# Fourier steps 48 to 127 as 64-row matmuls on both row halves, early maxima as head pairs among them

## The chip, the core and the metric

The program runs on one core of a Trainium2 chip. A core has TensorE (matmuls, with weight loads that run beside them; "PE" and "PEld" in the profile), VectorE (DVE), ScalarE (ACT), GpSimd (POOL) and SyncE (SP), which here only issues DMAs. TensorE writes to PSUM, eight banks of 128 x 512 floats; the other engines read PSUM (GpSimd does not here) and the on-chip memory. Each engine takes its instructions in the order of its own queue, and waits on semaphores for the others. The metric is the device time of one execution in microseconds, lower is better.

## What is computed

Two identical layers; each is a Fourier mixing block and then multi-query attention with 32 heads of 16 columns and one shared key and value head. S = 2048 rows, D = 512 columns.

```python
x = x + _A_ref(_layernorm(x), ...)      # a = x @ dft_hid_re.T ; b = x @ dft_hid_im.T
                                        # y = dft_seq_re @ a - dft_seq_im @ b
x = x + _B_ref(_layernorm(x), ...)      # q = x @ wq (32 heads) ; k = x @ wk ; v = x @ wv
                                        # softmax(q k^T / 4) v, then @ wo
```

The kernel does both blocks twice (two layers).

## The kernel before

**Precision.** A product of two float32 matrices is done in three matmuls on rounded parts: high x high, high x low, low x high (mm3, L86 to L89). Splitting a tile is a cast on ScalarE and a subtraction on VectorE or GpSimd (split_sb, split_ps, split_act, L70 to L84).

**The Fourier stage** (phase_a, L501) first multiplies along the sequence. There are four row blocks tb of 512 output rows, and for each block a cosine part (c = 0) and a sine part (c = 1) of 16 steps s: step n = 32 tb + 16 c + s multiplies the row tile s of the normalised input (xnh, xnl, kept for all 16 tiles) with a 128 x 512 tile of the cosine or sine matrix (ch, cl, loaded and split some steps ahead by c_load and c_split, four buffers each). The result has four 128-column parts d, each in a bank of its own (z, four banks from two pair() tiles); a step is four times mm3, twelve matmuls of 512 columns over all 128 rows. The last sixteen steps work on halves of 256 columns. After step 15 of a part the four z banks are split into zh and zl, and after both parts four y tiles of 128 rows (y_tile, L385: 24 matmuls into one y bank, then an add, a store and statistics on VectorE) finish the block.

**Preparing queries, keys and values.** While the next block's steps run, the twelve steps after a block's y tiles carry its preparation as tasks, one group behind each step (prep_tasks, L469): layer norm (alloc, ln_apply on GpSimd), four transposes (tr_tile, L246, into the single z-tagged bank, then split_act), keys and values (kv, L256), and four query projections (q_mm, L278), each with a weight split just ahead (wq_split) and six stores to DRAM (q_store). A query tile i (128 rows, 32 heads as 16 pairs) lies in DRAM as qd[i]: rows 0 to 63 belong to the even head of a pair and rows 64 to 127 to the odd one (48 rows used, 16 zero). qT_load brings it into one of the big buffers (slot) as o.qT[i].

**Maxima.** Softmax needs the row maximum of the scores of each head. For every query tile, pair, head g and key block kb of 512 keys this is one matmul (queries as weights, keys as the moving operand) into a y bank and one reduce_max on VectorE. There are three y banks (L65), shared with y_tile, kv, q_mm and the transposed maxima. Keys are kept twice: kz[0] has the keys on rows 0 to 63 and zeros below, kz[1] the other way round. In attention max_half (L344) uses the 64 rows of the head alone. In the Fourier stage max_one (L332) uses all 128 rows with the zero-padded kz[g], so that all matmuls there have one row mode. EARLY (L35) lists which (query tile, key block) is done in the Fourier stage: (i, kb, buffer, step of the load or None, begin, end). Begin and end are in units of which a block has 40: 32 steps, and 8 for its four y tiles (two per y tile, so a unit has four places both in steps and in y tiles). The 32 maxima of an entry are spread evenly over its units, put at quarters (after each d of a step, or after each three matmuls of a y tile; the dictionary inner).

**Attention** (phase_b, L833): per step four score matmuls of 64 rows (score, L681), their exponentials on ScalarE (L701), the product with the values (pv, L705) and on average three more maxima, taken from the list units, which leaves out what EARLY has done.

Of the kernel before, what the change touches and what calls it, by code (L numbers as in the profile page):

```python
# [17 lines left out]
P = 128  # L18
S = 2048
# [28 lines left out]
def fnet_mqa_kernel(ctx: ExitStack, tc: tile.TileContext, x_in, ct, dt_, wq, wkv, wo, out):  # L48
# [66 lines left out]
    def qd_zero(t):  # L115
        for g in range(2):
            nc.gpsimd.dma_start(qd[t, 64 * g + M0:64 * g + 64, :], f(kz[0][64:64 + 64 - M0, :]))
# [69 lines left out]
    def make_layer(L, src, mid, dst, last):  # L187
# [49 lines left out]
        def wq_split(g):  # L237
            st["wqh", g] = hl_tiles()
            split_sb(st["wq", g], *st["wqh", g], nc.gpsimd)
# [16 lines left out]
        def kv(t0, n, xth, xtl, vt=None):  # L256
            pk = bank("y")[:, :n * P]
            for k in range(NK):
                mm3(pk, wkvh[:, k, :], wkvl[:, k, :], xth[:, k, :n * P], xtl[:, k, :n * P], k == 0, k == NK - 1)
            cs = slice(t0 * P, (t0 + n) * P)  # L260
            if vt is None:
                vt = half(7)[:64, :n * P]
            nc.scalar.copy(vt[32:64], pk[32:64])
            for g in range(2):
                gs = slice(64 * g, 64 * g + 64)
                nc.scalar.activation(kz[g][gs, cs], pk[gs], AF.Identity, scale=kmask[gs], bias=kone[gs])
            for g in range(2):
                gs = slice(64 * g + 32, 64 * g + 48)
                nc.vector.tensor_sub(kz[g][gs, cs], pk[gs], f(kz[g][gs, cs]))
            return vt  # L270
# [61 lines left out]
        def max_one(i, pr, g, c0, n, to):  # L332
            pm = bank("y")[:, :n]
            nc.tensor.matmul(pm, o.qT[i][:, pr, :], kz[g][:, c0:c0 + n], start=True, stop=True)  # L334
            nc.vector.reduce_max(to, pm, axis=AX.X)  # L335

        def max_early(e, pr, g):
# [3 lines left out]
            to = st["mxe"][:, KEPT.index(EARLY[e]), pr, g:g + 1] if i else partial(0)[:, pr, g, kb:kb + 1]  # L341
            max_one(i, pr, g, kb * 512, 512, to)

        def max_half(i, pr, g, kb):  # L344
            pm = bank("y")
            gs = slice(64 * g, 64 * g + KR)
            nc.tensor.matmul(pm, o.qT[i][gs, pr, :], kz[g][gs, kb * 512:kb * 512 + 512], start=True, stop=True)  # L347
            nc.vector.reduce_max(partial(i)[:, pr, g, kb:kb + 1], pm, axis=AX.X)  # L348
# [120 lines left out]
        def prep_tasks(tb, x1):  # L469
# [20 lines left out]
            ts[5] = [do_kv]  # L490
            ts[6] = [lambda: wq_split(0), lambda: v_tr(4 * tb, 4, st["vt"])]
# [9 lines left out]
        def phase_a(extra):  # L501
# [8 lines left out]
            if L == 0:  # L510
                for n in range(NT):
                    add(n, lambda n=n: ln_step(n))
                add(20, load_wkv)
                for t in range(NT):
                    add(20 + 2 * t, lambda t=t: qd_zero(t))
# [5 lines left out]
            inner = {}  # L521
            for e, (i, kb, k, n0, n1, n2) in enumerate(EARLY):
                if n0 is not None:
                    add(n0, lambda i=i, k=k: qT_load(i, k))
                for u in range(2 * NPAIR):
                    at = divmod(int(4 * (n1 + u * (n2 - n1) / (2 * NPAIR))), 4)
                    b, n = divmod(at[0], 40)
                    at = (32 * b + n, at[1]) if n < 32 else ("y", b, 4 * (n - 32) + at[1])
                    inner.setdefault(at, []).append(lambda e=e, u=u: max_early(e, u // 2, u % 2))
            zh, zl, x1, vt = {}, {}, {}, {}  # L530
            z = None
# [15 lines left out]
            def maxes(c0, sl):  # L547
                for pr in range(HALF):
                    for g in range(2):
                        yield lambda pr=pr, g=g: max_one(0, pr, g, c0, 256, partial(0)[:, pr, g, sl:sl + 1])  # L550
# [33 lines left out]
            for n in range(125, 128):  # L584
                for d in range(NK):
                    inner[n, d] = [lambda: take(ma, 1)]
            add(124, lambda: wq_all(0))
            add(126, lambda: (wq_all(1), wq_split_pool(0), wq_split_pool(1)))
            add(127, lambda: (wq_split_pool(2), wq_split_pool(3)))
            for n in range(128):  # L590
# [3 lines left out]
                if s == 0:  # L594
                    za, zb = pair(), pair()
                    z = [za[:, 0, :], za[:, 1, :], zb[:, 0, :], zb[:, 1, :]]
                    if n == 112:
                        z = [z[d % 4][:, 256 * (d // 4):256 * (d // 4) + 256] for d in range(8)]
# [7 lines left out]
                ch, cl = hls.pop(n)  # L606
                for d in range(NK):
                    dsl = slice(d * P, (d + 1) * P)
                    if n < 112:
                        mm3(z[d], xnh[:, s, dsl], xnl[:, s, dsl], ch, cl, s == 0, s == NT - 1)  # L610
                        if s == 15 and d % 2:
                            for e in (d - 1, d):
                                raw = [half(6 + e % 2)] if c or e < d else []
                                (split_act if raw else split_ps)(z[e], zh[c][:, e, :], zl[c][:, e, :], *raw, neg=c == 1)
                    else:
                        h, sp = divmod(n - 112, 8)
                        zd = z[4 * h + d]
                        for j in range(2):
                            js = slice(256 * j, 256 * j + 256)
                            mm3(zd, xnh[:, 2 * sp + j, dsl], xnl[:, 2 * sp + j, dsl], ch[:, js], cl[:, js],  # L620
                                sp + j == 0, sp + j == 8)
                        if sp == 7 and d % 2:
                            hs = slice(256 * h, 256 * h + 256)
                            for e in (d - 1, d):
                                split_ps(z[4 * h + e], zh[c][:, e, hs], zl[c][:, e, hs], neg=c == 1)
                    for fn in inner.pop((n, d), ()):
                        fn()
# [24 lines left out]
            for g in range(4):  # L652
                q_half(14, g, *xt[1], lambda: take(mb, 2 if g else 0))
# [27 lines left out]
        def score(i, s_, j):  # L681
# [7 lines left out]
            if i == NT - 1 and jj == 1 and o.done == len(units):  # L689
                e = bank("y")  # L690
                nc.tensor.matmul(e, kz[g][64 * g:64 * g + KR, c * P:(c + 1) * P],
# [6 lines left out]
            nc.tensor.matmul(st["e"][:, g, :], kz[g][64 * g:64 * g + KR, c * P:(c + 1) * P],  # L698
# [248 lines left out]
```

## Time and profile before

| | us |
|---|---|
| median of three runs | 3772.63 (3770.57 to 3775.99) |
| the profiled execution, first to last instruction | 3768.5 |
| Fourier stage of layer 0, to step 44 / from step 45 | 190.76 / 513.94 |
| attention of layer 0 | 1185.90 |
| Fourier stage of layer 1, to step 44 / from step 45 | 177.50 / 509.90 |
| attention of layer 1 | 1190.50 |

One stretch of layer 0, the steps 76 to 95, with the busy time of each engine:

```profile
376.20:464.50 88.30, 86.51 (x370) 67.98 (x369) 81.36 (x133) 16.60 (x29) 28.65 (x23) 1.00 0.33 107
```

The row gives begin, end and length of the stretch, then for each engine in the order PE, PEld, DVE, ACT, POOL its busy us and number of instructions, then the clock that TensorE was granted (1.00 is full), the mean share of the DMA engines in use, and GB/s. In rows of the timeline the first two numbers are start and duration, then engine, source line, operation, out<-in, shape (rows * columns of the array for TensorE) and count; brackets hold the idle time of the engine before it and what ended it. A matmul's duration is longer than its slot, because matmuls are pipelined: the distance of starts is its cost.

### The profile page before, as it was taken

To read this page: it belongs to the slowest core of one execution; us is meant where nothing else is said; L and a number is where in the kernel's file an instruction comes from. 1 tells how busy PE (TensorE), PEld (TensorE's weight loads), DVE (VectorE), ACT (ScalarE), POOL (GpSimd) and SP (SyncE) were. 2 spreads that over 40 slices of the span, in tenths; PEclk is the share of its full clock that TensorE was granted. 3 is DMA by queue.
4 is the path that set the end of the run, shared out by engine and by line. 5 is a ranking of instruction groups with operands and counts; after the bars stand their busy time and mean duration, and the time that the engine had idled before them with its cause. 6 is when DMAs were issued, how large, how long until landed. Compare 5 with 4: busy or idle time off the path is not lost.

```text
span 3768.5 us, 56828 instructions
## 1 busy us (share of the span) xinstructions
PE 3662.8 (97%) x21826; PEld 1982.0 (53%) x21826; DVE 2804.0 (74%) x4743; ACT 2371.4 (63%) x2846; POOL 831.8 (22%) x1009
## 2 busy tenths in 40 slices
PE   8989999999999999999999999999999999999999
PEld 6777778633433333333377777785334333333433
DVE  5165978688888888888411769777888888888882
ACT  3212211588888888888933221216888888888888
POOL 5634342211111111111155343421000000000000
PEclk9999999999999999999999999999999999999999
DMA  5543332311111100110133342413111111001100
GB/s 181 122 136 103 99 97 88 98 34 37 42 35 33 50 21 21 33 49 21 41 129 103 112 126 76 123 60 99 33 49 32 35 35 44 24 21 49 33 23 25
DMA packets 204704, 242.51 MB, mean 64 GB/s; under 512 B 36880, under 2 KB 160784, under 8 KB 197264
## 3 DMA queue, kind: packets, MB, share of 16 engines
q1 hardware_dynamic: 199504, 222.08, 19.6%
q0 software_dynamic: 4864, 16.78, 1.6%
q8 instruction: 171, 2.80, 0.3%
q14 instruction: 101, 0.83, 0.1%
q10 hardware_dynamic: 64, 0.02, 0.0%
HBM read 174.58 MB, written 63.17 MB: 63 GB/s over the span
## 4 chain that ended last, share of the span: by engine, by line
PE 82%; DVE 4%; ACT 3%; issue 3%; POOL 2%; DMA 1%; SPq 0%; POOLq 0%; ACTq 0%; DVEq 0%
PE z L712 25%; PE x L698 18%; PE y L347 11%; PE y L334 6%; PE x L87 5%; PE x L89 5%; PE x L88 5%; PE y L87 3%; DVE mxp L348 3%; PE y L89 2%; PE y L88 2%; ACT slot L701 1%; POOL row L182 1%; POOL cl L79 1%; POOL slot L84 1%
## 5 line engine op out<-in xcount | busy, mean ns | idle before, releaser
L701 ACT ACTIVATE slot<-x 128x1024 f32<-128x1024 f32 x1990 | 1942.9, 1027 | 334.8 <-PE x L698 267.1
L348 DVE TENSOR_REDUCE mxp<-y 128x1 f32<-128x512 f32 x3040 | 1908.7, 684 | 280.6 <-PE y L347 228.4
L712 PE MATMUL z<-slot,v 128*32 128x512 f32 x8192 | 1096.2, 605 | 1.9 <-ACT row L715 1.9
L698 PE MATMUL x<-slot,kz 64*128 64x512 f32 x2956 | 900.4, 446 | 4.4 <-DMA slot<-mt 3.8
L698 PEld LDWEIGHTS x<-slot,kz 64*128 64x128 f32 x2956 | 375.1, 185 | 732.1 <-ACT slot L701 597.9
L347 PE MATMUL y<-kz,slot 64*128 64x512 f32 x2272 | 747.8, 436 | 4.7 <-ACT mt L378 0.7
L335 DVE TENSOR_REDUCE mxe<-y 128x1 f32<-128x512 f32 x832 | 525.2, 684 | 122.7 <-PE y L334 121.7
L87 PE MATMUL x<-ch,xnh 128*128 128x512 f32 (+1 forms) x1152 | 432.6, 376 | 12.9 <-ACT xnh L449 8.5
L89 PE MATMUL x<-ch,xnl 128*128 128x512 f32 (+1 forms) x1152 | 429.7, 373 | 1.2 <-POOL xnl L450 0.7
L88 PE MATMUL x<-cl,xnh 128*128 128x512 f32 (+1 forms) x1152 | 427.9, 371 | 0.4 <-POOL cl L79 0.4
L334 PE MATMUL y<-kz,slot 128*128 128x512 f32 (+1 forms) x1088 | 380.4, 399 | 43.6 <-DMA slot<-qd 15.3
L752 POOL TENSOR_TENSOR row<-row,row 128x256 f32<-128x256 f32 x63 | 46.2, 734 | 1679.6 <-DMA row<-rd 971.3
L347 PEld LDWEIGHTS y<-kz,slot 64*128 64x128 f32 x2272 | 359.3, 185 | 99.0 <-DVE mxp L348 29.6
L78 ACT CAST ch<-craw 128x512 fp32r<-128x512 f32 x256 | 156.4, 619 | 387.9 <-PE x L89 366.0
L79 POOL TENSOR_TENSOR cl<-craw,ch 128x512 fp32r<-128x512 f32 x236 | 307.8, 1310 | 361.4 <-ACT ch L78 295.4
L712 PEld LDWEIGHTS z<-slot,v 128*32 128x32 f32 x8192 | 163.5, 108 | 276.7 <-issue 248.6
L334 PEld LDWEIGHTS y<-kz,slot 128*128 128x128 f32 x1088 | 203.3, 190 | 106.6 <-DVE mxe L335 27.4
L87 PEld LDWEIGHTS x<-ch,xnh 128*128 128x128 f32 x1152 | 219.5, 191 | 52.9 <-ACT xnh L449 8.5
L88 PEld LDWEIGHTS x<-cl,xnh 128*128 128x128 f32 x1152 | 219.3, 190 | 43.5 <-POOL cl L79 0.7
L89 PEld LDWEIGHTS x<-ch,xnl 128*128 128x128 f32 x1152 | 218.7, 190 | 44.6 <-POOL xnl L450 4.5
L335 DVE TENSOR_REDUCE mxp<-y 128x1 f32<-128x512 f32 (+1 forms) x256 | 146.0, 619 | 126.5 <-PE y L334 125.8
L87 PE MATMUL y<-slot,slot 128*128 128x512 f32 x384 | 156.6, 408 | 8.9 <-DVE mxp L348 5.8
(144 smaller groups left out, 2837.3 us busy)
## 6 DMA issues: line engine op xcount, KB each, us to landing
craw<-ct_in SPq DMA_DIRECT2D x112, 512.0 KB
slot<-qd SPq DMA_DIRECT2D x44, 1024.0 KB
qd<-row SPq DMA_DIRECT2D x144, 128.0 KB
od<-row SPq DMA_DIRECT2D x252, 64.0 KB
row<-x_in SPq DMA_DIRECT2D x32, 256.0 KB
mid<-row POOLq DMA_DIRECT2D x32, 256.0 KB, 2.3
craw<-ct_in SPq DMA_DIRECT2D x32, 256.0 KB
row<-mid SPq DMA_DIRECT2D x32, 256.0 KB
```

Of the source, the lines that this page charges most:

```text
L78: nc.scalar.copy(hi, raw)
L79: (eng or nc.vector).tensor_sub(lo, raw, f(hi))
L87: nc.tensor.matmul(ps_, ah, bh, start=start, stop=False)
L88: nc.tensor.matmul(ps_, ah, bl, start=False, stop=False)
L89: nc.tensor.matmul(ps_, al, bh, start=False, stop=stop)
L334: nc.tensor.matmul(pm, o.qT[i][:, pr, :], kz[g][:, c0:c0 + n], start=True, stop=True)
L335: nc.vector.reduce_max(to, pm, axis=AX.X)
L347: nc.tensor.matmul(pm, o.qT[i][gs, pr, :], kz[g][gs, kb * 512:kb * 512 + 512], start=True, stop=True)
L348: nc.vector.reduce_max(partial(i)[:, pr, g, kb:kb + 1], pm, axis=AX.X)
L698: nc.tensor.matmul(st["e"][:, g, :], kz[g][64 * g:64 * g + KR, c * P:(c + 1) * P], o.qT[i][64 * g:64 * g + KR, cp:cp + 4, :], start=True, ...
L701: nc.scalar.activation(ptiles[i, s_][:, 2 * w:2 * w + 2, :], st.pop("e"), AF.Exp, scale=DH ** -0.5)
L712: nc.tensor.matmul(a[32 * j:32 * j + 32, :], v1[:, c, :], pt[:, j, :], start=c == 0, stop=c == NT - 1)
```

## The change

1. Steps 48 to 127: every 128-row matmul becomes two 64-row matmuls, one on rows 0 to 63 and one on rows 64 to 127, which go to different z banks (d and d + 2). Steps 48 to 111 are done two at a time (at the odd one): in a first phase one half of the rows goes into two of the banks and the other half into the other two, in a second phase the other way round. Between the phases ScalarE copies two values of a pair of banks (junk), so that the second phase waits until the first has written. Tasks of both steps follow at the end of the two. After each six matmuls (three slots of two) there is a place for early maxima (within).
2. An early maximum is done for both heads of a pair at once: two 64-row matmuls into two y banks, then two reductions (max_pair). The maxima of 256 columns at the end of the stage likewise.
3. Keys are kept once (kz), with head 0 on rows 0 to 63 and head 1 on rows 64 to 127. The room goes to one more query buffer, slot 9, whose first rows serve as the source of the zero rows before; these DMAs go six steps earlier.
4. EARLY is new: again sixteen entries, in another order and with other units; the first begins at unit 56 (step 48) instead of 53.5.
5. The split query weights get a buffer of their own (wqs, in slot 1), and the first of them is split one task group earlier, behind keys and values.

```diff
 EARLY = [
-    (0, 0, 2, 44, 53.5, 59.5), (1, 0, 3, 44, 59.5, 65), (2, 0, 2, 52, 65, 70.5), (3, 0, 8, 50, 70.5, 86),
-    (0, 1, 0, 66, 86, 90.5), (1, 1, 1, 66, 90.5, 94.5), (3, 1, 8, None, 94.5, 99.5),
-    (4, 0, 2, 78, 99.5, 104.5), (4, 1, 2, None, 104.5, 109.5), (5, 0, 8, 84, 109.5, 116),
-    (5, 1, 8, None, 116, 123), (6, 0, 0, 97, 123, 128), (6, 1, 0, None, 128, 133),
-    (7, 0, 2, 107, 133, 137.5), (7, 1, 2, None, 137.5, 142), (0, 2, 8, 101, 142, 147),
+    (2, 0, 2, 44, 56, 63), (3, 0, 3, 45, 63, 70), (0, 0, 8, 47, 70, 78), (1, 0, 9, 50, 78, 86),
+    (2, 1, 0, 65, 86, 91), (0, 1, 8, None, 91, 96.5), (1, 1, 9, None, 96.5, 102), (4, 0, 2, 79, 102, 107.5),
+    (6, 0, 8, 81, 107.5, 113), (6, 1, 8, None, 113, 118.5), (7, 0, 9, 87, 118.5, 123.5), (4, 1, 0, 96, 123.5, 128),
+    (7, 1, 9, None, 128, 133), (0, 2, 8, 97, 133, 138), (5, 0, 2, 107, 138, 142.5), (7, 2, 9, None, 142.5, 148),
 ]
...
-    kz = [sb.tile([P, S], F32R, name=f"kz{g}") for g in range(2)]
-    for g in range(2):
-        nc.gpsimd.memset(f(kz[g][64 * (1 - g):64 * (1 - g) + 64, :]), 0.0)
+    kz = sb.tile([P, S], F32R, name="kz")
+    junk = sb.tile([P, 2], F32, name="junk")
+    zero = slot(9)[:64 - M0, :]
+    nc.gpsimd.memset(zero, 0.0)
...
-            for g in range(2):
-                gs = slice(64 * g, 64 * g + 64)
-                nc.scalar.activation(kz[g][gs, cs], pk[gs], AF.Identity, scale=kmask[gs], bias=kone[gs])
+            nc.scalar.activation(kz[:, cs], pk, AF.Identity, scale=kmask, bias=kone)
...
-        def max_one(i, pr, g, c0, n, to):
-            pm = bank("y")[:, :n]
-            nc.tensor.matmul(pm, o.qT[i][:, pr, :], kz[g][:, c0:c0 + n], start=True, stop=True)
-            nc.vector.reduce_max(to, pm, axis=AX.X)
+        def max_pair(i, pr, c0, n, to):
+            pm = [bank("y")[:, :n], bank("y")[:, :n]]
+            for g in range(2):
+                gs = slice(64 * g, 64 * g + KR)
+                nc.tensor.matmul(pm[g], o.qT[i][gs, pr, :], kz[gs, c0:c0 + n], start=True, stop=True)
+            for g in range(2):
+                nc.vector.reduce_max(to[:, g:g + 1], pm[g], axis=AX.X)
...
-            ts[5] = [do_kv]
-            ts[6] = [lambda: wq_split(0), lambda: v_tr(4 * tb, 4, st["vt"])]
+            ts[5] = [do_kv, lambda: wq_split(0)]
+            ts[6] = [lambda: v_tr(4 * tb, 4, st["vt"])]
...
+            def z_rows(n, ops, m, cols, c):
+                sets = [((0, 1), (2, 3)), ((2, 3), (0, 1))]
+                for ph in range(2):
+                    half_of = sets[(m + ph) % 2]
+                    for dd in range(2):
+                        for j, (s, hl) in enumerate(ops):
+                            for t in range(3):
+                                for r in range(2):
+                                    d = half_of[r][dd]
+                                    rs_ = slice(64 * r, 64 * r + 64)
+                                    w = (xnl if t == 2 else xnh)[rs_, s, d * P:(d + 1) * P]
+                                    nc.tensor.matmul(z[d][:, cols], w, hl[j][t == 1][rs_], start=m == 0 and ph == 0 and j == t == 0,
+                                                     stop=j == 1 and t == 2 and (ph == 0 or m == 7), skip_group_check=True)
+                            within((n, 4 * ph + 2 * dd + j))
+                        if ph == 0:
+                            nc.scalar.copy(junk, zp[dd][:, :, cols.start])
+                        elif m == 7:
+                            evac(c, (dd, dd + 2), cols)
...
+                elif by_rows(n):
+                    if s % 2 == 0:
+                        continue
+                    hl = [hls.pop(n - 1), hls.pop(n)]
+                    z_rows(n - 1, [(s - 1, hl), (s, hl)], s // 2, slice(0, 512), c)
+                    for fn in tasks.pop(n - 1, ()):
+                        fn()
...
-                q_half(14, g, *xt[1], lambda: take(mb, 2 if g else 0))
+                q_half(14, g, *xt[1], lambda: take(mb, 1 if g else 0))
```

More of the change, by code (lines that the diff above doesn't have):

```diff
@@ L237, in wq_split @@
         def wq_split(g):
-            st["wqh", g] = hl_tiles()
+            if g == 0:
+                st["wqs"] = slot(1, F32R).rearrange("p (k n) -> p k n", k=4)
+            st["wqh", g] = [st["wqs"][:, 2 * (g % 2) + j, :] for j in range(2)]
             split_sb(st["wq", g], *st["wqh", g], nc.gpsimd)
@@ L524, in phase_a @@
                     add(n0, lambda i=i, k=k: qT_load(i, k))
[L525 to L529, printed above, removed]
+                for pr in range(NPAIR):
+                    b, n = divmod(int(4 * (n1 + pr * (n2 - n1) / NPAIR)), 160)
+                    n, k = divmod(n, 4)
+                    hook("y" if n >= 32 else 32 * b + n, b, 4 * (n - 32) + k if n >= 32 else k,
+                         lambda e=e, pr=pr: max_early(e, pr))
             zh, zl, x1, vt = {}, {}, {}, {}
-            z = None
             def view(ap, j):
@@ L548, in maxes @@
                 for pr in range(HALF):
-                    for g in range(2):
-                        yield lambda pr=pr, g=g: max_one(0, pr, g, c0, 256, partial(0)[:, pr, g, sl:sl + 1])
+                    yield lambda pr=pr: max_pair(0, pr, c0, 256, partial(0)[:, pr, :, sl])
             def take(it, n):
@@ L584, in phase_a @@
             for n in range(125, 128):
-                for d in range(NK):
-                    inner[n, d] = [lambda: take(ma, 1)]
+                for k in (1, 4, 6):
+                    inner[n, k] = [lambda: take(ma, 1)]
             add(124, lambda: wq_all(0))
@@ L589, in phase_a, with evac, within @@
             add(127, lambda: (wq_split_pool(2), wq_split_pool(3)))
+            def evac(c, ds, cols):
+                for k, d in enumerate(ds):
+                    if cols != slice(0, 512) or (k and not c):
+                        split_ps(z[d][:, cols], zh[c][:, d, cols], zl[c][:, d, cols], neg=c == 1)
+                    else:
+                        split_act(z[d], zh[c][:, d, :], zl[c][:, d, :], half(6 + k), neg=c == 1)
+            def within(at):
+                for fn in inner.pop(at, ()):
+                    fn()
[17 more added lines that the diff above has]
+                            evac(c, (dd, dd + 2), cols)
+            z = zp = None
             for n in range(128):
@@ L594, in phase_a @@
                 if s == 0:
[L595 to L598, printed above, removed]
+                    zp = [pair(), pair()]
+                    z = [zp[d % 2][:, d // 2, :] if by_rows(n) else zp[d // 2][:, d % 2, :] for d in range(4)]
                 if n in (26, 58, 90, 114):
@@ L605, in phase_a @@
                     zl[c] = slot(2 * c + 1, F32R).rearrange("p (k t) -> p k t", k=NK)
[L606 to L609, printed above, removed]
+                if n >= 112:
+                    ch, cl = hls.pop(n)
+                    h, sp = divmod(n - 112, 8)
+                    hl = [(ch[:, 256 * j:256 * j + 256], cl[:, 256 * j:256 * j + 256]) for j in range(2)]
+                    z_rows(n, [(2 * sp, hl), (2 * sp + 1, hl)], sp, slice(256 * h, 256 * h + 256), c)
+                elif by_rows(n):
+                    if s % 2 == 0:
[3 more added lines that the diff above has]
+                    for fn in tasks.pop(n - 1, ()):
+                        fn()
+                else:
+                    ch, cl = hls.pop(n)
+                    for d in range(NK):
+                        dsl = slice(d * P, (d + 1) * P)
                         mm3(z[d], xnh[:, s, dsl], xnl[:, s, dsl], ch, cl, s == 0, s == NT - 1)
                         if s == 15 and d % 2:
[L612 to L627, printed above, removed]
+                            evac(c, (d - 1, d), slice(0, 512))
+                        within((n, d))
                 for fn in tasks.pop(n, ()):
```

29 lines of the change are left out of this document (20 added, 9 removed).

## The prediction

> **What bounds the kernel now.** I read the page first, then the stretches of each stage (busy time by engine), then the timeline inside one stretch. The columns of a stretch are its length, then busy us and count for TensorE, its weight loads, VectorE, ScalarE and GpSimd, the granted clock and the DMA share.
>
> ```profile
> PE 3662.8 (97%) x21826; PEld 1982.0 (53%) x21826; DVE 2804.0 (74%) x4743; ACT 2371.4 (63%) x2846; POOL 831.8 (22%) x1009
> 0.00:190.76 190.76, 172.41 (x716) 134.47 (x717) 64.78 (x124) 65.91 (x121) 113.70 (x132) 0.99 0.55 152
> 190.76:704.70 513.94, 485.55 (x2321) 393.42 (x2319) 373.46 (x633) 111.28 (x204) 191.60 (x166) 0.98 0.33 101
> 704.70:1890.60 1185.90, 1173.92 (x7863) 462.26 (x7862) 991.00 (x1694) 1014.35 (x1111) 169.60 (x353) 1.00 0.13 38
> 1890.60:2068.10 177.50, 169.30 (x729) 134.26 (x729) 23.14 (x37) 55.63 (x95) 102.89 (x93) 1.00 0.38 118
> 2068.10:2578.00 509.90, 485.20 (x2324) 393.32 (x2322) 373.58 (x634) 111.28 (x204) 188.06 (x158) 0.99 0.32 100
> ...
> 2578.00:3768.50 1190.50, 1176.42 (x7880) 464.23 (x7877) 978.02 (x1622) 1012.97 (x1111) 65.94 (x111) 1.00 0.13 37
> ```
>
> The two long stretches (1185.9 and 1190.5 us) are attention; the change touches no work there, since it still leaves sixteen blocks of maxima to the Fourier stage, so I leave them as they are. What it touches is 513.94 us of layer 0 and 509.90 us of layer 1, from step 45 of the Fourier stage to its end. There TensorE is close to full and VectorE has slack (373 of 514 us). One piece of it:
>
> ```profile
> 240.23 0.40 PE L89 MATMUL x<-ch,xnl 128*128 128x512 f32 x1
> 240.46 0.39 PE L334 MATMUL y<-kz,slot 128*128 128x512 f32 x1
> 240.69 0.39 PE L87 MATMUL x<-ch,xnh 128*128 128x512 f32 x1
> 240.89 0.69 DVE L335 TENSOR_REDUCE mxe<-y 128x1 f32<-128x512 f32 x1 [0.21 <-PE y L334]
> 705.24 9.18 DVE L348 TENSOR_REDUCE mxp<-y 128x1 f32<-128x512 f32 x15 [0.24 <-PE y L347]
> ```
>
> A matmul over all rows takes the next slot every 0.23 us, and an early maximum costs one slot. Its reduction starts 0.43 us after it; fifteen in a row take 9.18 us, so VectorE needs 0.61 us each, 1.2 us for a head pair.
>
> **The Fourier steps as 64-row matmuls.** The attention stage shows such matmuls on both halves.
>
> ```profile
> 1001.57 0.39 PE L698 MATMUL x<-xnh,kz 64*128 64x512 f32 x1
> 1001.57 0.62 PE L347 MATMUL y<-kz,slot 64*128 64x512 f32 x2
> ...
> 1001.80 0.62 PE L698 MATMUL x<-xnh,kz 64*128 64x512 f32 x2
> ...
> L276 ACT COPY v<-z 128x64 f32<-128x64 f32 x3 | 0.6, 212 | 11.2 <-PE z L275 11.1
> ```
>
> Two start together, the next two 0.23 us later. So twice as many matmuls, two at a time, keep the pace, and I cost the steps themselves at nothing; trains in the trace are only three or four slots long, and what long ones do I keep for a rival. The two-column ScalarE copy between the phases is hidden: a small copy (last row) takes 212 ns, and six slots of the other two accumulators, 1.4 us (0.7 in the last sixteen steps), lie between it and the matmul that waits for it. Without that cover it would cost its 0.2 us and the way to and from ScalarE, some 0.5 us, 96 times.
>
> **What is saved.** Per layer 512 early maxima took 512 x 0.232 = 118.8 us; as 256 pairs they take half: **-59.4 us**. The smaller maxima of the last steps (256 columns) I leave at nothing: they save some 2 us and cross the row modes eight times.
>
> The first early maximum also waits for its queries.
>
> ```profile
> 201.82 1.22 PE L334 MATMUL y<-kz,slot 128*128 128x512 f32 x2 [8.80 <-DMA slot<-qd]
> 201.80:206.00 4.20, 4.18 (x10) 3.32 (x11) 1.98 (x3) 0.62 (x1) 0.88 (x1) 0.53 0.58 242
> PE y L334 <- DMA slot<-qd: 6.5, 1, 6.5
> ```
>
> 8.8 us in layer 0 and 6.5 in layer 1, and then some 4 us at a clock of 0.53, about 2 us lost. The first use moves from step 45.5 to 48, 7 us later, with the load still issued at step 44: about 1.6 us is left in layer 0, none in layer 1, **-8.7 us** on average. The other ten loads of queries only shift by some steps in SP's queue, each still three steps or more ahead of its use; the zero rows go six steps earlier through GpSimd's queue, 32 issues as before. Nothing for both.
>
> **What is added: waits for banks.** The ring has three banks. A single maximum needed one; a pair needs two, and both matmuls stand in TensorE's order ahead of the next Fourier chunk (six 64-row matmuls, 0.70 us). The second one waits until the previous pair's first reduction is over: 0.43 + 0.69 us and the signal, about 1.17 us after that pair, and one chunk plus a pair is only 0.70 + 0.23 = 0.93 us. And its weight load waits with it:
>
> ```profile
> 708.50 0.28 PEld L347 LDWEIGHTS y<-kz,slot 64*128 64x128 f32 x1 [0.32 <-DVE mxp L348]
> ```
>
> So pairs one chunk apart run at VectorE's 1.2 us, pairs two chunks apart at TensorE's 1.62 us, and the rest between is idle on one or the other. By the new table some 128 of the pairs outside the y tiles follow one chunk later. All of them at 1.2 instead of 0.93 us give +34 us; averaged over each entry (16 pairs in 4.5 units of 2.78 us against 19.2 us of VectorE, and so on) only +11 us. The halves may run one slot apart, which hides part. I take the middle: **+22 us**. Behind the waiting matmul stand the next chunk and, through it, ScalarE's next cast of a cosine tile, which has a step to spare.
>
> **Row modes among full-row matmuls.** The y tiles, transposes and projections stay at 128 rows. Attention shows the crossing, a pair among the output projection:
>
> ```profile
> 812.49 0.19 PEld L347 LDWEIGHTS y<-kz,slot 64*128 64x128 f32 x2 [0.37 <-issue]
> ...
> 812.92 0.50 PE L87 MATMUL y<-slot,slot 128*128 128x512 f32 x1
> 813.26 0.40 PE L88 MATMUL y<-slot,slot 128*128 128x512 f32 x1
> ...
> 814.20 0.39 PE L89 MATMUL y<-slot,slot 128*128 128x512 f32 x1
> 814.52 0.51 PE L347 MATMUL y<-kz,slot 64*128 64x512 f32 x2
> ```
>
> From one pair to the next, with six full matmuls between, 2.03 us; six slots are 1.40, so a pair costs 0.63 us there, of which 0.40 is the crossing there and back. The Trainium skill, "TensorEngine Tiling (Array Packing)", section Key Properties, says that changing the tiling mode drains the engine; this trace agrees, and by its 0.40 us a pair in a y tile is dearer than the two full-row maxima (0.46 us) that it replaces.
>
> By the table 39 pairs fall into the y tiles of a layer: 39 x 0.40 = 15.6 us. A y tile holds one bank itself, so pairs there have two: each must wait for both reductions before, and at a tile's end the add and the statistics come between on VectorE. Nothing to 16 us; I take 10: **+26 us**. Some 18 more crossings lie where projections and transposes follow a pair of steps: 18 x 0.40 = **+7 us**.
>
> **Prepared tiles come in twos.** Steps now run in pairs, and the tasks of both follow at the pair's end, one behind the other, where a step of matmuls lay between.
>
> ```profile
> 332.62 1.56 ACT L266 ACTIVATE kz<-y,kone,kmask 64x512 fp32r<-64x512 f32 x2
> 309.10 0.16 DVE L157 TENSOR_SCALAR lnv<-mv 128x4 f32<-128x4 f32 x1
> 310.61 2.07 POOL L182 TENSOR_SCALAR row<-row,mv,rs 128x512 f32<-128x512 f32 x1 [1.77 <-DVE rs L178]
> 312.74 0.66 PE L249 MATMUL z<-ident,row 128*128 128x128 f32 x4 [0.36 <-POOL row L182]
> 313.49 0.60 ACT L82 ACTIVATE row<-z 128x512 f32<-128x512 f32 x1 [3.48 <-PE z L249]
> 165.37 0.40 PE L87 MATMUL x<-ch,xnh 128*128 128x512 f32 x1
> 168.21 1.30 POOL L79 TENSOR_TENSOR cl<-row,ch 128x512 fp32r<-128x512 f32 x1
> 169.56 0.50 PE L89 MATMUL y<-slot,cl 128*128 128x512 f32 x1 [0.78 <-POOL cl L79]
> L82 ACT ACTIVATE row<-z 128x512 f32<-128x512 f32 x12 | 7.2, 598 | 34.2 <-PE z L249 34.2
> L83 ACT CAST slot<-row 128x512 fp32r<-128x512 f32 x32 | 19.9, 621 | 1.2
> L84 POOL TENSOR_TENSOR slot<-row,slot 128x512 fp32r<-128x512 f32 x32 | 41.3, 1298 | 44.0 <-ACT slot L83 43.7
> ```
>
> The layer norm's chain runs from 309.10 to the first transpose at 312.74, 3.6 us under a step of matmuls now and in the open then. A projection ends at 165.37; the next one's third matmul, which needs a weight split only then, comes at 169.56: 4.2 us later instead of 0.5. Key and value behind the last transpose wait for 0.6 + 0.62 + 1.3 us. The second of two transposes waits about 1 us for the single z bank. Together 3.6 + 3.7 + 2.5 + 1 = 10.8 per prepared block, less some 2 us of such waits now (0.4 at 312.74, 0.8 at 169.56), two blocks per layer, with a slow clock perhaps behind the longest: 8 to 24, I take **+20 us**. Keys in one activation instead of two (1.56 us) save 0.8 us in there, within the rounding.
>
> **The sum.** -59.4 - 8.7 + 22 + 26 + 7 + 20 = +6.9 us per layer, +14 us: the profiled span goes from 3768.5 to about 3782. The median of the runs shown, 3772.6, lies 4 us above that span, so **3786 us**.
>
> **Rivals.**
> *Banks are not waited for* (ends faster). Place: the ring of three banks. The halves may run a slot apart and the second matmul of a pair then never meets an unread bank; the two bank terms fall to 11 and 16. -59.4 - 8.7 + 11 + 16 + 7 + 20 = -14 per layer, 3744 us. For it: 0.93 us is only 0.24 short of 1.17. Against: the row at 708.50, where each matmul waits for VectorE once it is full. It decides if pairs in steps 80 to 96 come at under 1.25 us on average.
> *Merged tasks are covered* (no change). GpSimd and ScalarE may have run ahead; 10 instead of 20 gives -3 per layer, 3767 us. Against: the layer norm's first operation stands behind the last reduction on VectorE.
> *Long trains of 64-row matmuls are slower.* A layer has 960 slots of them (64 steps of 12, and 16 of 24 at half length). At 0.25 us instead of 0.232 they cost 17 us more: 3821 us. At the bound above, 0.34 us, the gap from 812.92 to 813.26 right behind a crossing, they cost 104 us more per layer: 3993 us. For it: twice the instructions; against: the rows at 1001.57 and 1001.80. The Trainium skill, "TensorE: Matmul & The Clock Gate", Part 3, has four packed row tiles at 3.07 times the speed of one; two halves at that efficiency would take 0.30 us a slot and the kernel some 130 us more, an estimate from that page, which the 0.23 us here speak against.
> *The halves don't overlap.* Then a layer takes some 220 us more, above 4200 us; the same two rows speak against it.
>
> **Chances.** Forecast 0.45, banks 0.27, covered 0.15, trains at 0.25 us 0.10, at 0.34 us 0.02, no overlap 0.01. A measurement here can tell 0.2%, about 7.5 us. The forecast's own spread is 3770 to 3810; with the bank rival below and the trains at 0.25 us above the range is 3736 to 3826. Faster 0.34, same 0.18, slower 0.48.
>
> **What would show it.** The four y tiles of block 2 now:
>
> ```profile
> 464.50:499.40 34.90, 33.61 (x136) 24.31 (x135) 29.76 (x48) 3.42 (x6) 6.22 (x7) 1.00 0.14 53
> ```
>
> Pairs one chunk apart at 1.2 us, with weight loads released by VectorE; this stretch over 40 us; the first transpose of a block idle for 3 us or more; two Fourier matmuls starting together every 0.23 us. I am wrong if that last pace fails, or if TensorE's waits for VectorE stay small between steps 80 and 96.

## The result, and the profile after

| | before | after |
|---|---|---|
| median, four runs each (us) | 3774.27 (3770.57 to 3775.99) | 3801.94 (3799.45 to 3804.91) |
| profiled execution, first to last instruction (us) | 3768.5 | 3803.1 |

The changed kernel is slower: 1.0075 times the time before, 95% interval 1.0061 to 1.0090, or 27.7 us, some 14 us per layer. The forecast was slower by 14 us in all.

First the stretches of the stages of the changed kernel, cut at the same points of the program as those of before (columns as there: length, busy us and count for TensorE, weight loads, VectorE, ScalarE and GpSimd, then the granted clock, DMA share and GB/s).

```profile
0.00:192.10 192.10, 170.81 (x718) 132.69 (x719) 64.61 (x124) 65.14 (x120) 114.80 (x137) 1.00 0.57 155
192.10:720.60 528.50, 491.65 (x3472) 354.84 (x3470) 368.88 (x634) 121.02 (x296) 187.47 (x160) 0.96 0.31 97
720.60:1904.80 1184.20, 1174.29 (x7863) 462.34 (x7862) 990.75 (x1693) 1014.30 (x1111) 169.08 (x352) 1.00 0.13 38
1904.80:2082.70 177.90, 169.70 (x731) 134.59 (x731) 22.09 (x37) 55.28 (x95) 103.10 (x93) 1.00 0.40 118
2082.70:2611.40 528.70, 491.80 (x3472) 354.42 (x3470) 368.86 (x633) 120.92 (x296) 186.35 (x158) 0.96 0.31 96
2611.40:3803.10 1191.70, 1176.83 (x7882) 464.54 (x7880) 977.96 (x1623) 1012.92 (x1111) 65.76 (x111) 1.00 0.13 37
```

Attention is where it was (1184.2 and 1191.7 us, 1185.9 and 1190.5 before). The loss sits in the two stretches from step 45: 528.5 instead of 513.9 us, 528.7 instead of 509.9. VectorE, ScalarE and GpSimd have nearly the same work there as before (369 against 373 us for VectorE), so the loss is not added work on one of them; TensorE's own stretch is longer, and its granted clock fell from 0.98 and 0.99 to 0.96.

Next the timeline of TensorE within a pair of steps (start, length, engine, line, operation).

```profile
401.10 0.61 PE L629 MATMUL x<-ch,xnh 64*128 64x512 f32 x2
401.33 0.61 PE L629 MATMUL x<-cl,xnh 64*128 64x512 f32 x2
...
401.80 0.62 PE L336 MATMUL y<-kz,slot 64*128 64x512 f32 x2
402.02 0.62 PE L629 MATMUL x<-ch,xnh 64*128 64x512 f32 x2
```

Two matmuls every 0.23 us, and a head pair takes the place of one slot: long trains of 64-row matmuls keep the pace of the full rows, and the saving per pair is real. So the loss is in waits and crossings. TensorE's weight loads at the early maxima wait for VectorE 244 times in the changed kernel, 1.5 us at the longest. The page has these waits in the row of the weight loads, over both layers, for before and after (busy, mean ns | idle before, and the part of it that the largest releaser ended):

```profile
L334 PEld LDWEIGHTS y<-kz,slot 128*128 128x128 f32 x1088 | 203.3, 190 | 106.6 <-DVE mxe L335 27.4
```

```profile
L336 PEld LDWEIGHTS y<-kz,slot 64*128 64x128 f32 x1088 | 180.8, 187 | 146.8 <-DVE mxe L338 90.2
```

Idle time of the weight loads is not all lost (they overlap the matmuls), but its cause changed: 27.4 us for VectorE before, 90.2 us now. The maxima that go to the tile mxp add 8.9 us before and 25.1 now. The y tiles of blocks 1 and 2, the first row of before (block 2's stands in the prediction), the others of after:

```profile
279.70:305.70 26.00, 26.00 (x114) 21.15 (x113) 15.50 (x26) 3.84 (x7) 6.65 (x7) 1.00 0.08 31
```

```profile
257.30:291.50 34.20, 34.20 (x131) 20.27 (x128) 24.76 (x43) 4.48 (x8) 6.74 (x7) 1.00 0.15 54
453.30:497.60 44.30, 41.93 (x143) 22.49 (x142) 33.81 (x56) 3.56 (x7) 5.80 (x7) 1.00 0.16 59
```

8.2 and 9.4 us longer. Last the preparation of block 2: TensorE's timeline at the first transpose, at two merged query projections, and at keys and values (with the early maximum behind them).

```profile
298.32 0.39 PE L629 MATMUL x<-ch,xnl 64*128 64x512 f32 x1
302.70 1.12 PE L251 MATMUL z<-ident,row 128*128 128x128 f32 x4 [3.99 <-POOL row L182]
...
304.34 0.63 PE L629 MATMUL x<-cl,xnh 64*128 64x512 f32 x2
304.77 0.63 PE L629 MATMUL x<-ch,xnl 64*128 64x512 f32 x2
```

```profile
354.60 0.39 PE L88 MATMUL y<-slot,slot 128*128 128x512 f32 x1
356.90 0.50 PE L86 MATMUL y<-slot,slot 128*128 128x512 f32 x1 [1.92 <-ACT slot L77]
...
359.01 0.74 PE L88 MATMUL y<-slot,slot 128*128 128x512 f32 x1 [1.38 <-POOL slot L78]
359.55 0.63 PE L86 MATMUL y<-slot,slot 128*128 128x512 f32 x1
```

```profile
323.07 0.49 PE L86 MATMUL y<-slot,wkvh 128*128 128x512 f32 x1 [1.40 <-ACT slot L82]
324.44 0.50 PE L87 MATMUL y<-slot,wkvh 128*128 128x512 f32 x1 [0.88 <-POOL slot L83]
...
331.04 0.49 PE L336 MATMUL y<-kz,slot 64*128 64x512 f32 x1 [1.34 <-DVE kz L269]
```

The transposes wait 4 us for the layer norm, the second projection 1.9 and 1.4 us for its weight split, keys and values 1.4 and 0.9 us, and the early maximum behind them 1.3 us for the keys. Behind these waits the slots come every 0.42 us instead of 0.23. The granted clock in four such stretches of this block (the third number from the end of each row):

```profile
304.20:308.00 3.80, 3.80 (x20) 2.96 (x20) 1.29 (x2) 2.13 (x5) 3.21 (x4) 0.51 0.00 0
324.40:328.50 4.10, 4.06 (x11) 3.16 (x11) 0.00 (x0) 0.00 (x0) 0.00 (x0) 0.58 0.34 134
331.70:335.00 3.30, 3.23 (x16) 2.54 (x18) 2.48 (x5) 0.27 (x2) 2.95 (x3) 0.52 0.00 0
359.10:362.70 3.60, 3.60 (x9) 2.86 (x10) 0.00 (x0) 0.00 (x0) 0.00 (x0) 0.53 0.94 182
```

14.8 us at about half speed: some 7 us lost in one block, beside the waits themselves. One of the four, behind the wait for the keys, is not the change's: the kernel before waits 2.3 us for the keys at the same place, and its clock is 0.58 in the 4.1 us behind that. So some 5 us of the 7 are new.

### The profile page after: what moved, and what is told of

It is laid out like the page before. It is cut to its first block, busy times and chain, and to the rows that moved or that the text cites. A ratio compares the mean times of both kernels' runs of the same rounds, so it can differ in the third digit from the quotient of the medians.

```text
span 3803.1 us, 61730 instructions
## 1 busy us (share of the span) xinstructions
PE 3675.1 (97%) x24130; PEld 1903.4 (50%) x24130; DVE 2793.1 (73%) x4743; ACT 2389.6 (63%) x3028; POOL 826.6 (22%) x1008
## 5 line engine op out<-in xcount | busy, mean ns | idle before, releaser
L629 PE MATMUL x<-ch,xnh 64*128 64x512 f32 (+1 forms) x1536 | 429.4, 383 | 7.4 <-DVE slot L74 5.6
L629 PE MATMUL x<-ch,xnl 64*128 64x512 f32 (+1 forms) x1536 | 399.0, 359 | 0.0
L629 PE MATMUL x<-cl,xnh 64*128 64x512 f32 (+1 forms) x1536 | 398.7, 359 | 0.0
L350 PEld LDWEIGHTS y<-kz,slot 64*128 64x128 f32 x2208 | 349.6, 185 | 94.1 <-DVE mxp L351 27.4
L336 PE MATMUL y<-kz,slot 64*128 64x512 f32 (+1 forms) x1088 | 376.7, 431 | 17.5 <-DVE mxe L338 6.4
L633 ACT COPY junk<-x 128x2 f32<-128x2 f32 x192 | 30.6, 159 | 390.0 <-PE x L629 296.1
L629 PEld LDWEIGHTS x<-cl,xnh 64*128 64x128 f32 x1536 | 252.1, 190 | 20.5
L629 PEld LDWEIGHTS x<-ch,xnl 64*128 64x128 f32 x1536 | 251.1, 189 | 22.0
L629 PEld LDWEIGHTS x<-ch,xnh 64*128 64x128 f32 x1536 | 236.5, 189 | 35.8 <-issue 11.5
L336 PEld LDWEIGHTS y<-kz,slot 64*128 64x128 f32 x1088 | 180.8, 187 | 146.8 <-DVE mxe L338 90.2
L86 PE MATMUL y<-slot,slot 128*128 128x512 f32 x480 | 208.0, 433 | 17.4 <-ACT slot L77 7.7
```

The costliest lines, as they stand in the source:

```text
L86: nc.tensor.matmul(ps_, ah, bh, start=start, stop=False)
L336: nc.tensor.matmul(pm[g], o.qT[i][gs, pr, :], kz[gs, c0:c0 + n], start=True, stop=True)
L350: nc.tensor.matmul(pm, o.qT[i][gs, pr, :], kz[gs, kb * 512:kb * 512 + 512], start=True, stop=True)
L629: nc.tensor.matmul(z[d][:, cols], w, hl[j][t == 1][rs_], start=m == 0 and ph == 0 and j == t == 0, stop=j == 1 and t == 2 and (ph == 0 or ...
```

## The experiments

The effect of an edit is given per layer, as half the difference of two medians; the 95% intervals reach some 5 us to each side of a median, so such a number is good to about 3 us.

**The first load of queries, alone, in the kernel before** (the table's first entries begin 2.5 units later, the third is loaded three steps later).

```diff
-    (0, 0, 2, 44, 53.5, 59.5), (1, 0, 3, 44, 59.5, 65), (2, 0, 2, 52, 65, 70.5), (3, 0, 8, 50, 70.5, 86),
+    (0, 0, 2, 44, 56, 62), (1, 0, 3, 44, 62, 67), (2, 0, 2, 55, 67, 72), (3, 0, 8, 50, 72, 86),
```

> The kernel before, with the first early maximum at step 48 instead of 45.5 and the first three entries of the table a little closer together; the loads stay where they are, but for the third, issued at step 55 instead of 52. Theory (the first maximum waits for its queries, 8.8 and 6.5 us and some 2 us of slow clock): 7 to 9 us less per layer, 3757 to 3760 us, without a single 64-row step. Rival (the wait moves to another load or to VectorE): no change, 3774 us within 8.

Measured 3757.0 us, 0.9957 of before (0.9945 to 0.9970): 15.1 us, or 7.6 per layer. What TensorE and its weight loads waited for at the early maxima (us, times; one wait can count for both), in the kernel before and in this one:

```profile
  DVE mxe L335: 37.5, 70
  DMA slot<-qd: 31.5, 4
```

```profile
  DVE mxe L335: 39.3, 75
...
  DMA slot<-qd: 1.0, 2
```

The wait for the load is gone and no other took its place. This part of the change's gain needs no 64-row step.

**The tasks of a pair's first step between its two phases.**

```diff
@@ z_rows
                         if ph == 0:
                             nc.scalar.copy(junk, zp[dd][:, :, cols.start])
                         elif m == 7:
                             evac(c, (dd, dd + 2), cols)
+                    if ph == 0 and n < 112:
+                        for fn in tasks.pop(n, ()):
+                            fn()
@@ the loop over steps
                     z_rows(n - 1, [(s - 1, hl), (s, hl)], s // 2, slice(0, 512), c)
-                    for fn in tasks.pop(n - 1, ()):
-                        fn()
```

> The changed kernel, but the tasks of the first step of each pair run between its two phases instead of behind the whole pair; nothing else is moved. Theory (tasks in twos leave their waits uncovered): in layer 0 the changed kernel waits some 27 us at transposes, key/value and query projections (5.1 and 4.2 us before the first transposes, 2.1 + 1.5 us in each pair of projections, and so on) and some 8 us at the slow clock behind them; most of it goes, and five more crossings of the row mode per block cost 10 x 0.40 = 4 us per layer: 23 to 30 us less per layer, 3742 to 3756 us. By the size on record (20 us per layer): 3770 us. Rival (the waits are for producers that are late anyway, GpSimd and VectorE): no change, 3802 us within 8.

Measured 3742.8 us, 0.9921 of before (0.9908 to 0.9935), 59.1 us below the changed kernel: 29.6 per layer, the theory. The first transpose of block 2, TensorE's waits for the layer norm at the transposes (us in total over both layers, times, longest; the changed kernel, then this one), and the whole stretch from step 45:

```profile
298.90 0.66 PE L251 MATMUL z<-ident,row 128*128 128x128 f32 x4 [0.39 <-POOL row L182]
```

```profile
PE z L251 <- POOL row L182: 24.8, 10, 4.8
```

```profile
PE z L251 <- POOL row L182: 6.9, 7, 2.2
```

```profile
192.10:688.30 496.20, 477.99 (x3469) 345.29 (x3467) 369.02 (x633) 120.95 (x295) 187.17 (x158) 1.00 0.33 103
```

0.39 us of wait where there were 3.99, and the granted clock is back from 0.96 to 1.00. With keys, values and projections the list has 55.9 us of such waits in the changed kernel and 12.6 here, 21.6 per layer less; the kernel before has 14.7. One slow stretch is left in this block, behind a wait of 1.33 us for the keys at 320.47:

```profile
322.50:325.90 3.40, 3.40 (x17) 2.25 (x13) 2.77 (x5) 0.25 (x2) 1.57 (x2) 0.50 0.20 52
```

The rest of the change, with its tasks apart again, is faster than the kernel before.

**No pairs in the y tiles.** In both runs those pairs are left out, with their maxima; in the first GpSimd writes the constant in their place, in the second VectorE.

```diff
                 if n == "y":
-                    at = "y", b, k
+                    return
...
                 st["mxe"] = sb.tile([P, len(KEPT), NPAIR, 2], F32, name="mxe")
+                nc.gpsimd.memset(st["mxe"], -1e30)
```

> The changed kernel without the early head pairs that fall into the y tiles (39 per layer by the table; their maxima are left out, the partial maxima start from a constant, and the exponent is scaled by a sixteenth so that it stays finite). Theory (a pair among full-row matmuls pays the crossing and a bank wait): 39 x (0.23 + 0.40) + 10 = 35 us per layer by the record, 3733 us; by the trace of the changed kernel, where 39 pairs cost 8.2 + 12.8 = 21 us above their slots, 30 us per layer, 3742 us. Rival (only their slots count, the crossing is hidden): 9 us per layer, 3784 us.

Measured 3741.9 us (0.9917 of before, 0.9904 to 0.9931): 30.0 per layer. But the edit had a price of its own, as the timeline at its first pairs shows:

```profile
203.60 2.50 POOL L78 TENSOR_TENSOR cl<-craw,ch 128x512 fp32r<-128x512 f32 x2
...
206.02 0.46 POOL L346 MEMSET mxe<- 128x416 f32 x1
...
206.51 2.48 DVE L340 TENSOR_REDUCE mxe<-y 128x1 f32<-128x512 f32 x4 [3.01 <-POOL mxe L346]
...
207.26 0.79 PE L338 MATMUL y<-kz,slot 64*128 64x512 f32 x1 [4.17 <-DVE mxe L340]
```

The write waited its turn on GpSimd (two operations, 2.5 us), the reductions for it, and TensorE for their banks.

> As the run without the pairs in the y tiles, but the constant is written by VectorE instead of GpSimd: there the write stood behind two GpSimd operations, the first reductions waited for it (3.0 us, then TensorE 4.2 us, and slots of 0.43 us behind them), and the stretch up to the first y tiles was 5.7 us longer than in the changed kernel. The y tiles themselves were 34 us per layer shorter (34.2 to 22.2 and 44.3 to 22.1 us). Theory: 34 us per layer, 3734 us. Rival (the 30 us measured are the whole price, the wait was there otherwise): 3742 us.

Measured 3731.7 us (0.9892, 0.9876 to 0.9909): 35.1 per layer. The y tiles of this run:

```profile
259.55:281.75 22.20, 22.20 (x100) 17.96 (x98) 5.37 (x11) 4.49 (x8) 6.75 (x7) 1.00 0.17 62
443.35:465.45 22.10, 22.00 (x97) 17.94 (x96) 6.03 (x12) 3.49 (x7) 5.74 (x7) 1.00 0.18 59
```

The slots of 39 pairs are 39 x 0.232 = 9.0 us, so 26 us per layer are crossing and banks, the size of the forecast. The rival falls.

**Reductions of half the width, after and before.** Only VectorE's time per early maximum changes: 419 ns (row below) where the prediction's rows have 0.69 us (the maxima of the other 256 keys are left out).

```diff
-                nc.vector.reduce_max(to[:, g:g + 1], pm[g], axis=AX.X)
+                nc.vector.reduce_max(to[:, g:g + 1], pm[g][:, :256], axis=AX.X)
```

> The changed kernel, with the reductions of the early head pairs over the first 256 of their 512 columns (the other half of those keys is left out of the maxima; the exponent is scaled by a sixteenth so that it stays finite). The matmuls are the same. Theory (a pair waits for its second bank until VectorE has read the pair before): the waits of the pairs go, 22 us per layer in the steps and some 10 in the y tiles by the record: 64 us less, 3738 us. Rival (TensorE's own reload after a pair is what costs, not VectorE): no change, 3802 us within 8.

> The kernel before, with the reductions of its early maxima over the first 256 of their 512 columns (the other half of those keys is left out of the maxima; the exponent is scaled by a sixteenth so that it stays finite). It tells how much of the 70 us that the same edit took from the changed kernel the kernel before had too. Theory (VectorE's waits grew with the change): layer 0 of before shows some 10 us of waits for VectorE at its maxima, so 8 to 10 us per layer, 3753 to 3758 us, and the change's own part is 25 us per layer. Rival (the waits were there all along): some 35 us per layer, 3704 us.

Measured: the changed kernel falls to 3731.9 us (0.9889, 0.9874 to 0.9904), 35.0 per layer; the kernel before to 3758.0 (0.9960, 0.9946 to 0.9974), 7.6 per layer. So some 27 us per layer are waits for VectorE that the change brought. The reductions, TensorE's weight loads and the y tiles with half-width reductions in the changed kernel:

```profile
L338 DVE TENSOR_REDUCE mxe<-y 128x1 f32<-128x256 f32 x832 | 313.8, 419 | 302.4 <-PE y L336 278.7 <-PE x L629 23.6
L336 PEld LDWEIGHTS y<-kz,slot 64*128 64x128 f32 x1088 | 164.1, 188 | 61.2 <-issue 21.4 <-DVE mxe L338 16.5 <-DVE mxp L338 3.4
```

```profile
256.00:289.00 33.00, 33.00 (x129) 20.12 (x128) 16.46 (x42) 4.37 (x8) 6.67 (x7) 1.00 0.15 55
442.00:480.60 38.60, 37.57 (x145) 21.08 (x143) 21.58 (x56) 4.07 (x7) 6.35 (x7) 1.00 0.16 58
```

The waits for VectorE fall from 90.2 to 16.5 us. In the y tiles the half width takes 34.2 - 33.0 + 44.3 - 38.6 = 6.9 us. The kernel before loses part of that too: its y tiles with half-width reductions are

```profile
282.60:308.50 25.90, 25.90 (x113) 21.02 (x112) 11.30 (x26) 3.70 (x7) 6.50 (x7) 1.00 0.08 31
465.40:498.40 33.00, 32.27 (x135) 24.84 (x134) 19.64 (x47) 3.28 (x6) 6.07 (x7) 1.00 0.15 56
```

and so 26.0 - 25.9 + 34.9 - 33.0 = 2.0 us shorter. Of the 27 us some 5 are then bank waits in the y tiles and 22 lie in the steps. Of these at most 1.5 are something else that a faster VectorE helps, the layer norm: the waits for it at the transposes go from 24.8 to 21.7 us in both layers together.

What is left of the changed kernel's y tiles at half width, above the tiles without pairs and above the slots, is 33.0 + 38.6 - 22.2 - 22.1 - 9.0 = 18.3 us for 39 pairs, 0.47 us a pair: the crossing, with some rest of bank waits, since in block 2 the weight loads at the pairs still wait 4.4 us for VectorE. Block 1, where they don't, gives (33.0 - 22.2 - 16 x 0.232) / 16 = 0.44 us a pair.

**Fewer blocks of early maxima, none in a y tile.** Both have the tasks between the phases. The new tables spread fourteen or twelve blocks over the steps 48 to 123, and attention's allowance of maxima grows by one every six or three steps:

```diff
-            return min(3 * (n + 1) + 12 + o.extra, len(units)) - o.done
+            return min(3 * (n + 1) + n // 6 + 12 + o.extra, len(units)) - o.done
```

> The kernel with the tasks between the phases, and a new table: fourteen blocks of early maxima instead of sixteen, none in a y tile, evenly over the steps from 48 to 123; the attention stage takes the 64 maxima more (one more every six steps of its loop). Theory (a pair in a y tile costs 0.53 us above its slot, 39 of them 21 us per layer; a pair in attention costs its slot only): 42 us less than with the tasks moved alone, 3701 us within 8. Rival (the maxima moved to attention make VectorE, busy 991 of 1186 us there, the bound, or the pairs in the steps stand closer and wait more for banks): 3743 us or more.

> As the one with fourteen blocks, but twelve blocks: 192 pairs per layer, 1.6 chunks apart on average, and 128 more maxima per layer in attention (one more every three steps of its loop), where VectorE then has about 991 + 128 x 0.62 = 1070 us of work in 1200. Theory (each pair one chunk behind another waits some 0.27 us for a bank; about 80 pairs do so instead of about 140): 60 x 0.27 = 16 us per layer below the one with fourteen blocks, 3669 us within 15. Rival (VectorE bounds attention): as the one with fourteen, or slower, with attention longer by more than 128 slots of 0.12 us = 15 us per layer.

Measured 3767.9 us (0.9984, 0.9975 to 0.9993) and 3804.9 (1.0081, 1.0067 to 1.0095): the rival, both times, in its first half, for it is attention that is longer (rows below).

**More blocks.** The same tasks; a seventeenth block, one pair behind each chunk of the two y tiles at step 119, and an eighteenth in the table; attention's allowance falls by one every sixteen or eight steps.

> The kernel with the tasks between the phases, and seventeen blocks of early maxima: the old sixteen (the last three in another order) and one more, a pair after each chunk of the two y tiles at step 119; attention has 32 maxima less per layer. Theory, from the runs with fourteen and twelve blocks (32 pairs fewer in the stage made it 31 and 21 us shorter, 64 maxima more made attention 43 us longer): a maximum in attention costs 0.68 us, VectorE's time for it, so a pair 1.36; in a y tile a pair costs 0.76. 16 x 0.6 = 10 us less per layer: 3743 - 19 = 3724 us. Rival (attention is at another bound with sixteen, ScalarE or TensorE, and gets no shorter): 16 x 0.76 = 12 us more per layer, 3767 us.

> As the one with seventeen blocks, but eighteen: from step 70 on the pairs of the table stand a chunk apart nearly throughout, and attention has 64 maxima less per layer than with sixteen. Theory: a pair put between two that are two chunks apart costs 2 x 1.2 - 1.62 = 0.78 us, 1.36 in attention: 9 us less per layer than with seventeen, 3705 us. Rival (VectorE's other work in the stage and the banks make such a pair as dear as one in attention): as with seventeen or slower, 3724 us or more.

Measured 3783.5 us (1.0034, 1.0020 to 1.0049) and 3829.6 (1.0150, 1.0137 to 1.0163): no gain either time, as the rivals said, but the first is 16.5 us above its rival's 3767. The attention stretch of layer 0 with sixteen, fourteen, twelve, seventeen and eighteen blocks, each from its kernel's own run:

```profile
688.40:1873.70 1185.30, 1173.96 (x7863) 462.28 (x7862) 990.87 (x1693) 1014.48 (x1111) 169.66 (x352) 1.00 0.13 38
```

```profile
657.10:1885.80 1228.70, 1208.13 (x7927) 475.42 (x7926) 1027.84 (x1757) 1015.46 (x1114) 168.77 (x350) 1.00 0.13 37
```

```profile
635.90:1907.30 1271.40, 1242.17 (x7992) 487.53 (x7990) 1066.04 (x1821) 1014.74 (x1114) 168.93 (x348) 1.00 0.12 36
```

```profile
712.00:1890.90 1178.90, 1171.45 (x7832) 457.35 (x7830) 971.97 (x1661) 1012.64 (x1111) 168.57 (x348) 1.00 0.13 38
```

```profile
726.90:1915.15 1188.25, 1174.36 (x7799) 452.94 (x7798) 952.74 (x1629) 1012.71 (x1112) 168.72 (x349) 0.99 0.13 38
```

With 64 maxima more attention is 43.4 us longer, with 128 more 86.1: 0.68 us each, the time of one reduction on VectorE, although VectorE is idle for 16% of that stretch. With 32 fewer it is only 6.4 us shorter, 0.2 each, and with 64 fewer 3 us longer (TensorE waits there once, 5.5 us, for a load of queries), while the Fourier stage before it ends 23.6 and 38.5 us later. So of these tables sixteen blocks is the knee: above it a pair in the Fourier stage is nearly pure cost, below it attention pays 1.36 us a pair. Why attention pays the whole reduction while VectorE has idle time wasn't settled. The two y tiles at step 119 also show what a pair behind every chunk costs, first without (the kernel with the tasks moved alone), then with sixteen pairs:

```profile
610.65:621.80 11.15, 11.15 (x50) 8.94 (x48) 4.15 (x9) 1.04 (x3) 0.61 (x1) 1.00 0.07 25
```

```profile
615.95:643.20 27.25, 25.25 (x80) 12.19 (x78) 22.51 (x39) 1.04 (x3) 0.61 (x1) 1.00 0.03 12
```

1.0 us each, slot included.

**Sixteen blocks, none in a y tile.** Since attention wants sixteen, the last kernel keeps them (and attention as it was) and puts all 256 pairs into the steps 48 to 123, the tasks between the phases.

```diff
-    (2, 0, 2, 44, 56, 63), (3, 0, 3, 45, 63, 70), (0, 0, 8, 47, 70, 78), (1, 0, 9, 50, 78, 86),
...
+    (2, 0, 2, 44, 48, 53.5), (3, 0, 3, 45, 53.5, 59), (0, 0, 8, 47, 59, 64.5), (1, 0, 9, 50, 64.5, 70),
+    (2, 1, 0, 65, 70, 74.5), (0, 1, 8, None, 74.5, 79), (1, 1, 9, None, 79, 83.5), (4, 0, 2, 79, 83.5, 88),
+    (4, 1, 2, None, 88, 92.5), (6, 0, 8, 81, 92.5, 97), (6, 1, 8, None, 97, 101.5), (7, 0, 9, 87, 101.5, 106),
+    (7, 1, 9, None, 106, 110.5), (5, 0, 2, 107, 110.5, 115), (0, 2, 8, 102, 115, 119.5), (7, 2, 9, None, 119.5, 124),
```

(Begin and end are steps here.)

> The kernel with the tasks between the phases, with sixteen blocks as there, but none of them in a y tile: 256 pairs in the 304 chunks of the steps 48 to 123. Attention keeps its maxima. Theory (39 pairs leave the y tiles, at 0.76 us each, and stand between two that were two chunks apart, at 0.78): no change, 3743 us within 8; from the one with fourteen blocks, whose stage ended at 656.9 us in layer 0, 32 pairs more at 0.78 give 682 against 688, up to 12 us less. Rival (a run of pairs one chunk apart over most of the stage is held by VectorE, which also has the layer norms and the splits to do): 1.36 a pair, 16 us per layer more, 3775 us.

Measured 3729.5 us, 0.9882 of before (0.9869 to 0.9896): 13.3 us below the table with pairs in y tiles. That is more than the 8 us allowed around no change, and about the second figure, 12 us less. Of the kernels that leave nothing out it is the fastest, 44 us below the kernel before and 72 below the changed one.

## Why the prediction held, and where it was short

The direction came from the right mechanisms; the size was half of what came. The sign hung on little, +6.9 us as the remainder of -68 and +75. The +22 for the banks in the steps was the middle between 11 and 34, taken without a reason for the middle; that it was met is luck. Per layer, in the order of the prediction's sum (the last column says which runs):

| term | forecast | measured | from |
|---|---|---|---|
| 256 pairs for 512 maxima | -59.4 | not measured by itself; 0.23 us a pair slot | timeline |
| wait for the first queries | -8.7 | -7.6 | run on the kernel before |
| bank waits, steps and y tiles | +22 and +10 | +27 together: 22 and 5 | half-width reductions, after less before |
| crossing in y tiles | +15.6 | +17 to +18 | half width against no pairs |
| crossings elsewhere | +7 | not measured by itself | |
| tasks in twos | +20 | +29.6, or 34 with the crossings it paid | tasks between the phases |
| sum | +6.9 | +15 (or +19) with the two terms not measured as forecast; 13.8 by the medians | |

**Saving and query load.** Right. The trains of 64-row matmuls, kept as a rival at 0.25 us or more, stay at 0.23 over whole pairs of steps, and the wait for the load went without a successor. The 0.30 us a slot that the prediction estimated from the Trainium skill's packing figure ("TensorE: Matmul & The Clock Gate", Part 3) isn't there: two halves together take the 0.23 us of one full-row matmul.

**Banks.** The mechanism is shown: make VectorE's reduction shorter and change nothing else, and 35 us per layer go, most of which the kernel before did not have. The rival that banks are not waited for falls; the mark set for it was under 1.25 us for a pair between steps 80 and 96. The steps 76 to 95 of the changed kernel:

```profile
374.20:452.80 78.60, 77.35 (x598) 54.13 (x597) 71.96 (x117) 21.41 (x52) 29.89 (x24) 1.00 0.43 138
```

By the table 58 pairs lie in it (5.5 units for 16): 1.36 us a pair, where TensorE's own pace would be 1.375 x 0.70 + 0.23 = 1.19. That is above the mark.

**Row modes in the y tiles.** 26 us forecast; the changed kernel has 26 above the slots. But the kernel before had some 4 us of waits there too (60.9 - 44.3 - 54 x 0.232 for its 54 maxima), so some 22 are the change's: the crossing is 0.44 to 0.47 us a pair rather than 0.40, the bank waits 5 us rather than 10. A pair there, 0.23 + 0.44 and its share of the waits, is dearer than the two full-row maxima (0.46 us) that it replaced.

**Tasks in twos: the term that was too small.** It was put at 20 us, 10.8 of waits per block less 2, with "a slow clock perhaps behind the longest". That is 17.6 us of waits per layer, and some 2 for the clock. The waits came nearly as worked out: 28.0 us per layer in the list against 7.4 before, so 20.6. What was too small is the slow clock, which in the rows above follows each wait of 1.3 us and more, and not only the longest. Moving the tasks apart took 29.6 us, with five more crossings per block paid for in it (some 4 us per layer at 0.40 each, an estimate from the prediction's row), so the term was 30 to 34: 21.6 of waits, and 8 to 12 for the clock. The rival of covered tasks falls. The Trainium skill, "TensorE: Matmul & The Clock Gate", Part 1 (HAM oscillation), warns of TensorE gaps above about 3.4 us; here waits of 1.3 to 1.9 us have slow stretches behind them, one of them (at 320.47 in the run with the tasks between the phases) with no other wait above 0.4 us in the 20 us before it, and the measurement decides.

The measured terms, with the two others as forecast, sum to +15 us per layer, or +19 with 34 for the tasks, against 13.8 by the medians; each is good to some 3 us only. A gain that the sum left in the rounding is not among them: TensorE's waits for the keys at the early maxima fell from 11.6 to 4.3 us in both layers together, 3.7 per layer. The startup is 1.3 us longer in the profiled execution (192.10 against 190.76 to step 45). The kernel before varies as much without the change: in the run with half-width reductions, which differs only behind that point, its last matmul of step 44 starts at 192.18 instead of 190.53.

## What to carry to other kernels

When two iterations are fused, look at what was hidden in the seam between them: here the tasks that lay behind each step lost their cover, and the short waits cost half as much again because the matmul clock dropped behind each. Putting one half of the tasks back into the middle turned a loss of 0.75% into a gain of 0.8%, both against the kernel before. Halving TensorE's work on something that VectorE must read back is only worth it where VectorE can follow: count the consumer's time per item and the buffers between before counting the saving.

## What the runs showed of the hardware

- Pairs of 64-row matmuls on the two row halves run at 0.23 us a pair of 512 columns over long trains, the slot of one full-row matmul.
- A pair of them between full-row matmuls costs 0.44 us beyond its slot where no bank is waited for (7.1 us for 16 pairs).
- The granted clock falls to 0.50 to 0.58 for 3.3 to 4.1 us behind TensorE waits as short as 1.3 to 1.9 us.
- One write of a small tile by GpSimd (0.46 us) ahead of the first reductions cost TensorE 4.2 us, since it stood behind two 1.25-us operations of its engine's queue.
- In attention one more maximum costs 0.68 us, its reduction's own time, with VectorE 84% busy; 32 fewer gain 0.2 us each, and 64 fewer nothing.
